# A triangular inverse whose blocks are turned on VectorE instead of through HBM, with a few mixture pieces moved into the next block

## The chip, the cores and the metric

The kernel runs on one core of a Trainium2 chip. The time is the device time of one execution in microseconds (us). The fast runs of one kernel in the same rounds lie 0.1 to 0.7% apart. Every run compared here is marked fast in the record (mean granted clock 0.932 to 0.963), or is the single run of a look without rounds, which is marked as such. The granted clock is the profile's figure for the share of full speed granted to TensorE; "slow clock" below means a stretch in which it is under 1 and the same work takes longer (0.68 over 518.9 to 525.6 us of the kernel before, where a ph piece takes 6.64 us instead of 4.51). Engines are named as in the profile: PE is TensorE's matmuls, PEld its weight loads, DVE is VectorE, ACT ScalarE, POOL GpSimd, SP SyncE; a name with q (SPq) is that engine's sequencer, for instance while it issues a transfer. "L481" is line 481 of the kernel that the profile belongs to, so the same code has other line numbers in other kernels.

## The reference

A recurrent attention (8 heads of 40, batch 4, 768 time steps) is followed by a mixture of four experts.

```python
for t in range(S):                                    # S = 768, per (batch, head)
    y[:, :, t] = einsum('bhd,bhde->bhe', r_t, state)
    Sa = einsum('bhde,bhe->bhd', state, a_t)
    state = state * w_t - einsum('bhd,bhe->bhde', Sa, b_t) + einsum('bhd,bhe->bhde', v_t, k_t)
x = y, as rows (B*S, H*D) = (3072, 320)
p = domain_probs / domain_probs.sum(-1)               # 4 experts
out = sum over e of  p[:, e] * (relu(x @ w1[e]) @ w2[e])    # w1: 320x1024, w2: 1024x320
```

## The kernel before

Time is cut into 12 chunks of 64 steps. Inside a chunk the recurrence is solved with a unit-triangular 64x64 inverse for each batch and head; state passes from chunk to chunk. The chunks are worked on in seven blocks (1, 2, 2, 2, 2, 2 and 1 chunks); a chunk has two units (half the batch each). A block does, in PE's order, which is the program's order (the scheduler orders the other engines; in e9 below pieces written ahead of the solve moved only one of VectorE's evictions):

1. per unit: turn the inputs (`pW`, `pNK`, `pKN`, `pA`, `pR`), make the triangles (`pef`), turn back (`pkn`);
2. `solve()`: up to 128 inverses of 32x32 triangles on VectorE, one per lane;
3. `inverse()`: join the 32x32 inverses to 64x64 ones (`pi`, `px`);
4. the steps of the chunks (`pa` ... `py`), and the result to HBM and back as `xT`.

The mixture of the block before is cut into pieces, `ph` (wide, x @ w1) and `po` (narrow, h @ w2), that are laid between these stages: `mix(us)` adds credit, and pieces run as far as the credit goes.

The triangles lie with rows on partitions, and `solve()` wants one triangle per lane. So they go through HBM:

```python
    def load(x, u):                    # the five inputs; each nat tile has ONE buffer
        ...
                nc.sync.dma_start(out=n[:, :, 0:D], in_=src[0].rearrange("h t e -> t h e"))
    def triangles(u):
        ...
            nc.scalar.copy(out=u.q.F[half(s), u.x], in_=cut(pef[s][half(s)]))
        ...
                nc.sync.dma_start(out=u.q.FD[s, z, ...].rearrange("m r t -> r m t"),     # to HBM
                    in_=blocks(u.q.F, s, z)[...])
    # in attention(), once the block's triangles are there:
                nc.sync.dma_start(out=Gl[u.q.lanes, 0:Q * Q], in_=u.q.FD[:]...)            # from HBM, by lanes
    def inverse(q, x):
        if x == 0:
            for y, t in enumerate((Xl, Tl)):
                nc.sync.dma_start(out=XD[y]..., in_=t[q.lanes, 0:Q * Q])                   # to HBM
            for s in range(2):
                for z in range(2):
                    nc.sync.dma_start(out=blocks(xt, s, z)[:, 0:n], in_=XD[0, s, z]...)    # from HBM, by rows
                nc.sync.dma_start(out=blocks(q.F, s, 0)[:, 0:n], in_=XD[1, s, 0]...)
        ...                                                                                # pi, px on TensorE

    def weights(e):                    # one buffer each for w1s and w2s
        ...
                nc.gpsimd.dma_start(out=w1s[half(d)], ...)
            nc.gpsimd.dma_start(out=w2s[:], ...)
    def narrow(e, tt):
        po = mbank("po")               # the mixture has four PSUM banks in turn
        ...                            # matmuls, then VectorE evicts po into osb

    def mix(us):
        if not queue and ahead:
            stage(*ahead.pop(0))
        credit[0] += us * credit[1]
        while queue and credit[0] >= queue[0][0] / 2:
            t, piece = queue.pop(0)
            credit[0] -= t
            piece()

    def attention(b):
        us = b.units
        stage(us[0], 1)                                  # decays: pW
        for y, u in enumerate(us):
            stage(u, 2)                                  # scaled: pNK, pKN, pA
            if y + 1 < len(us):
                stage(us[y + 1], 1)
            mix(4.3)
            stage(u, 3)                                  # triangles: pef
            mix(2.2)
            stage(u, 4)                                  # natural: pkn, pR
        ...
        solve(b.n * NP * 4 * M)
        mix(56)
        ...                                              # inverse, steps with mix, gather

    for y, b in enumerate(all_blocks):
        credit[:] = [0.0, sum(t for t, _ in queue) / 137]
        attention(b)
        mix(1e9)                                         # what is left of the mixture runs here
        queue += mixture(b.cs, b.xT)
    mix(1e9)
```

## Time and profile before

| | before |
|---|---|
| time, median of 3 runs | 1415.08 us (1414.68 to 1415.97) |
| span of the profiled run, TensorE's mean granted clock | 1413.4 us, 0.963 |
| busy: PE, DVE, ACT | 1255.5, 592.3, 262.8 us |
| moved by DMA | 135.75 MB |

PE's busy share, in tenths, in 40 equal slices of the span (35.3 us each):

```profile
PE   4167878978999978999978999979899979999998
```

The first nine slices are blocks 0 and 1, where PE waits most. After that each block shows one dip (7 or 8): the start of the block, where PE waits for the inputs. TensorE is 89% busy, so every gain has to come out of these dips or out of slow-clock stretches. The prediction shows the waits themselves.

### The profile page before, as it was taken

The numbers are of one execution on the slowest core, as the hardware profiler recorded it, in microseconds if no ns is written. First come the engines' busy times: TensorE is split into PE (matmuls) and PEld (weight loads), VectorE is DVE, ScalarE is ACT, GpSimd is POOL, SyncE is SP. The second block draws the span as 40 slices with busy tenths as digits, with TensorE's granted clock in tenths as the row PEclk, the third lists the DMA queues.
The fourth block names the chain that finished last, engine by engine and source line by source line (L and its number), as shares of the span: only waits on it lengthen the run. The fifth ranks groups of instructions, "written<-read, shape, count | busy, mean of one in ns | idle before, by whom it ended". The sixth has DMA issues, their size and how long they took to land.

```text
span 1413.4 us, 26645 instructions
## 1 busy us (share of the span) xinstructions
PE 1255.5 (89%) x11680; PEld 874.3 (62%) x11680; DVE 592.3 (42%) x877; ACT 262.8 (19%) x521; POOL 75.2 (5%) x108
## 2 busy tenths in 40 slices
PE   4167878978999978999978999979899979999998
PEld 4166656856557756557755657656557665566676
DVE  7744572345623345623345443345452335612000
ACT  1021212112121203111203112203113202120111
POOL 3000000000000000000000000000000000000010
PEclk9997988889999989999989999989999999999999
DMA  8233654456353446354445353354462353414363
GB/s 135 44 57 73 115 137 106 82 113 105 91 118 80 90 105 95 82 123 95 85 108 94 81 127 70 91 125 85 93 127 58 85 133 65 93 46 103 93 148 86
DMA packets 284020, 135.75 MB, mean 96 GB/s; under 512 B 246977, under 2 KB 265473, under 8 KB 283905
## 3 DMA queue, kind: packets, MB, share of 16 engines
q1 hardware_dynamic: 266304, 60.60, 24.6%
q0 software_dynamic: 17600, 73.46, 21.1%
q8 instruction: 92, 1.51, 0.5%
q14 instruction: 24, 0.19, 0.0%
HBM read 116.70 MB, written 17.30 MB: 95 GB/s over the span
## 4 chain that ended last, share of the span: by engine, by line
PE 70%; DMA 13%; DVE 10%; SPq 4%; issue 2%; ACT 1%; POOL 0%; DVEq 0%; ACTq 0%
PE ph L481 26%; PE po L493 23%; DVE tmp L288 3%; DMA natW<-in_w_dram 3%; PE pc L418 3%; PE pef L218 3%; DMA natKN<-in_b_dram 2%; DMA natA<-in_a_dram 2%; DMA w1s<-in_moe_w_dram 2%; SPq L162 2%; PE pa L379 2%; PE py L430 2%; PE pt L389 2%; PE py L436 1%; PE pSN L351 1%
## 5 line engine op out<-in xcount | busy, mean ns | idle before, releaser
L481 PE MATMUL ph<-xT,w1s 64*128 64x512 f32 (+1 forms) x2240 | 455.5, 553 | 18.1 <-DVE osb L502 8.1
L493 PE MATMUL po<-w2s,hs 128*128 128x320 f32 x1536 | 430.1, 437 | 0.0
L493 PEld LDWEIGHTS po<-w2s,hs 128*128 128x128 f32 x1536 | 289.4, 191 | 122.6 <-issue 8.5
L481 PEld LDWEIGHTS ph<-xT,w1s 64*128 64x128 f32 x2240 | 226.7, 196 | 210.1 <-issue 182.1
L487 ACT ACTIVATE hs<-ph 128x512 f32<-128x512 f32 (+1 forms) x224 | 110.4, 534 | 623.9 <-PE ph L481 623.0
L502 DVE SCALAR_TENSOR_TENSOR osb<-po,gate,osb 128x320 f32<-128x320 f32 x72 | 39.1, 549 | 370.1 <-PE po L493 370.1
L191 DVE RECIPROCAL GI<-G 128x512 f32<-128x512 f32 x24 | 80.5, 3353 | 0.8
L467 POOL DMA_DIRECT2D w1s<-in_moe_w_dram x56 | 37.8, 679 | 770.2 <-PE ph L481 770.2
L168 PE MATMUL pW<-ident,natW 128*128 128x128 f32 x96 | 18.6, 327 | 50.1 <-DMA natW<-in_w_dram 45.5
L329 PE MATMUL pi<-F 32*32 32x32 f32 x768 | 16.5, 199 | 47.0 <-DMA F<-XD 47.0
L218 PEld LDWEIGHTS pef<-AE,KNT 64*128 64x128 f32 x768 | 50.2, 199 | 12.6 <-issue 11.4
L471 POOL DMA_DIRECT2D w2s<-in_moe_w_dram x28 | 26.0, 928 | 545.7 <-PE po L493 545.7
L288 DVE TENSOR_TENSOR tmp<-Xl,Gl 128x1024 f32<-128x1024 f32 (+5 forms) x49 | 54.2, 1107 | 0.9
L225 DVE TENSOR_TENSOR AE<-pef,mask 64x512 f32<-64x512 f32 x48 | 33.1, 689 | 51.1 <-ACT F L223 50.3
L186 DVE TENSOR_TENSOR_SCAN G<-w_shift,first 128x520 f32<-128x520 f32 x24 | 29.8, 1242 | 56.1 <-ACT w_shift L184 55.9
L218 PE MATMUL pef<-AE,KNT 64*128 64x64 f32 x768 | 51.3, 283 | 2.2 <-DVE AE L205 2.1
L418 PEld LDWEIGHTS pc<-R,VST 64*128 64x128 f32 x768 | 47.8, 199 | 6.8 <-issue 4.2
L418 PE MATMUL pc<-R,VST 64*128 64x64 f32 x768 | 48.9, 284 | 2.0 <-DVE VST L357 1.4
L184 ACT COPY w_shift<-pW 128x512 f32<-128x512 f32 x24 | 14.0, 585 | 192.0 <-PE pW L168 189.5
L329 PEld LDWEIGHTS pi<-F 32*32 32x32 f32 x768 | 15.0, 115 | 52.0 <-issue 44.7
L168 PEld LDWEIGHTS pW<-ident,natW 128*128 128x128 f32 x96 | 13.1, 166 | 54.0 <-issue 48.1
L223 ACT COPY F<-pef 64x512 f32<-64x512 f32 x48 | 27.8, 580 | 99.5 <-PE pef L218 98.9
(104 smaller groups left out, 1013.7 us busy)
## 6 DMA issues: line engine op xcount, KB each, us to landing
w1s<-in_moe_w_dram POOLq DMA_DIRECT2D x56, 640.0 KB, 8.1
w2s<-in_moe_w_dram POOLq DMA_DIRECT2D x28, 1280.0 KB, 7.3
xT<-yD SPq DMA_DIRECT2D x24, 320.0 KB
natW<-in_w_dram SPq DMA_DIRECT2D x48, 80.0 KB
natA<-in_a_dram SPq DMA_DIRECT2D x48, 80.0 KB
natR<-in_r_dram SPq DMA_DIRECT2D x48, 80.0 KB
yD<-Yo SPq DMA_DIRECT2D x48, 80.0 KB
out_dram<-osb SPq DMA_DIRECT2D x48, 80.0 KB
```

What stands on the lines that cost most here:

```text
L168: nc.tensor.transpose(out=p[:, j * P:(j + 1) * P], in_=nat[x][:, 2 * j:2 * j + 2, :].rearrange("p h e -> p (h e)"), identity=ident[:],)
L191: nc.vector.reciprocal(out=u.GI[:], in_=u.G[:, :, 1:L + 1])
L218: nc.tensor.matmul(out=pef[s][:, m * L:(m + 1) * L], lhsT=KNT[half(s), m].rearrange("p x t -> p (x t)"), rhs=u.AE[half(s), s, m, :], start ...
L225: nc.vector.tensor_tensor(out=u.AE[o, s], in0=cut(pef[s][o]), in1=mask[o, None, :].to_broadcast([64, M, L]), op=ALU.mult,)
L288: nc.vector.tensor_tensor(out=m, in0=in0[:, :, None, :].to_broadcast([P, n0, n1, nr]), in1=in1[:, None, :, :].to_broadcast([P, n0, n1, nr] ...
L329: nc.tensor.matmul(out=p[hi, at], lhsT=f[lo, m, Q:L], rhs=f[lo, m, 0:Q], start=True, stop=True, tile_position=(SL[s], SL[s] + Q),)
L418: nc.tensor.matmul(out=pc[s][:, m * L:(m + 1) * L], lhsT=VST[half(s), i, j * P:(j + 1) * P], rhs=u.R[half(s), m, :], start=True, stop=True,)
L467: nc.gpsimd.dma_start(out=w1s[half(d)], in_=moe_w1[e, :, d * (F // 2):(d + 1) * (F // 2)].rearrange("(k p) f -> p k f", p=64),)
L481: nc.tensor.matmul(out=ph[d][:, 0:n], lhsT=w1s[half(d), k_, f * P:(f + 1) * P], rhs=xT[half(d), k_, 0:n], start=(k_ == 0), stop=(k_ == NK ...
L487: nc.scalar.activation(out=hs[-1][1][:, 0:n], in_=ph[d][:, 0:n], func=ACTF.Relu)
L493: nc.tensor.matmul(out=po[:, 0:DM], lhsT=h[:, tt * P:(tt + 1) * P], rhs=w2s[:, f, :], start=(x == 0), stop=(x == NF - 1),)
L502: nc.vector.scalar_tensor_tensor(out=osb[tt][:], in0=po[:, 0:DM], scalar=sc, in1=osb[tt][:], op0=ALU.mult, op1=ALU.add,)
```

## The change

Its intent is to take the four trips through HBM away. VectorE's transposition, as the changed kernel uses it, turns 32x32 blocks for every 32 partitions: with one triangle column per turn, it moves rows to lanes and back. `Tl`'s way back falls away, since F gets X as it is and XT gets it turned. Five other things came with it: the inputs KN and R of the first chunk are issued from ACT, the first weights wait for a tile of block 0, block 1's first two `decays` are written ahead of block 0's solve (before, all stages of these units were spread over block 0's steps), `VST` stands ahead of `pd` in a step, and not all mixture pieces run at the end of a block: some 13 us of them, three narrow pieces, stay for the next block. The core of the diff (renamings and the reshaping of `solve` are cut):

```diff
 def load(x, u):
+            by = nc.scalar if u.c == 0 and x in ("KN", "R") else nc.sync
 def triangles(u):
-            nc.scalar.copy(out=u.q.F[half(s), u.x], in_=cut(pef[s][half(s)]))
+            for z in range(2):
+                r = slice(SL[s] + z * Q, SL[s] + (z + 1) * Q)
+                nc.scalar.copy(out=F_[r, u.m, 0:L - z * Q], in_=cut(pef[s][r])[:, :, z * Q:L])
-        for s in range(2):
-            for z in range(2):
-                nc.sync.dma_start(out=u.q.FD[...], in_=blocks(u.q.F, s, z)[...])
+    def columns(t):
+        return t[:, :, 0:Q].rearrange("p m t -> p t m")
 def solve():
+        nc.vector.transpose(out=square(Gl), in_=columns(F_))
 ...
+        nc.vector.transpose(out=columns(F_), in_=X)
+        for z in range(2):
+            nc.vector.transpose(out=columns(XT[:, :, z * Q:L]), in_=X.rearrange("p r t -> p t r"))
+        for s in range(2):
+            nc.gpsimd.memset(XT[SL[s] + Q:SL[s] + L, :, 0:Q], 0.0)
 def inverse(u, x):
-        if x == 0:
-            ...                                       # XD to HBM and back
 def step(u, yD):                                      # VST moved ahead of pd
 def weights(e):
+            if cs[0] == e == 0:
+                for t in (w1s, w2s):
+                    nc.gpsimd.tensor_copy(out=t[:, 0, 0:1], in_=all_blocks[0].units[1].KNT[:, 0, 0, 0:1])
 def mix(us):
-        if not queue and ahead:
-            stage(*ahead.pop(0))
 def attention(b, after):
         if b.cs[0] == 0:
             ...
+            for u in after.units[0:NP]:
+                stage(u, 1)
-            ahead.extend((u, upto) for u in all_blocks[1].units[0:NP] for upto in range(1, 5))
 for y, b in enumerate(all_blocks):
-        mix(1e9)
+        credit[:] = [sum(t for t, _ in queue) - 13, 1.0]
+        mix(0)
         queue += mixture(b.cs, b.xT)
-    mix(1e9)
+    credit[0] = 1e9
+    mix(0)
```

More of the change, by code (lines that the diff above doesn't have):

```diff
@@ L115 @@
     VS = [const.tile([P, 2, NJ, 2, 64], FP32, name=f"VS{p}_") for p in range(NP)]
-    XT = [const.tile([P, 2, M, L], FP32, name=f"XT{p}_") for p in range(NP)]
+    F_ = const.tile([P, 2 * NP * M, L], FP32, name="F")
+    XT = const.tile([P, 2 * NP * M, L], FP32, name="XT")
     DG = 8 * (Q + 1)
     Xl, Tl, Gl = (const.tile([P, 4 * DG], FP32, name=x) for x in ("Xl", "Tl", "Gl"))
+    nc.gpsimd.memset(F_[:], 0.0)
+    for t in (Xl, Tl):
+        nc.gpsimd.memset(t[:], 0.0)
     def clear():
-        for t in (Xl, Tl):
+        for t in RV + VS:
             nc.gpsimd.memset(t[:], 0.0)
@@ L126, in clear @@
             nc.gpsimd.memset(t[:, Q + 1:Q + 1 + (Q - 1) * (Q + 1)].rearrange("p (a c) -> p a c", c=Q + 1)[:, :, 0:1], 1.0)
-        for t in XT + RV + VS:
-            nc.gpsimd.memset(t[:], 0.0)
     gate = const.tile([P, NC, NP, E], FP32, name="gate")
@@ L157, in load @@
             src = [y[2 * u.p + i, :, u.t, :] for y in srcs[x]]
+            by = nc.scalar if u.c == 0 and x in ("KN", "R") else nc.sync
             if srcs[x][0] is srcs[x][1]:
-                nc.sync.dma_start(out=n[:, :, 0:D], in_=src[0].rearrange("h t e -> t h e"))
+                by.dma_start(out=n[:, :, 0:D], in_=src[0].rearrange("h t e -> t h e"))
                 continue
             for s in range(2):
-                nc.sync.dma_start(out=n[:, s::2, 0:D], in_=src[s][s::2].rearrange("h t e -> t h e"))
+                by.dma_start(out=n[:, s::2, 0:D], in_=src[s][s::2].rearrange("h t e -> t h e"))
     def turn(x):
@@ L209, in triangles @@
     def triangles(u):
-        KNT, q = u.KNT, u.q
-        if q.F is None:
-            q.F = sb.tile([P, 2, M, L], FP32, name="F", tag="F", bufs=2)
-            q.FD = hbm.tile([2, 2, q.n * M, Q, Q], FP32, name="FD", tag="FD", bufs=4)
+        KNT = u.KNT
         pef = [bank("pef") for _ in range(2)]
@@ L227, in triangles @@
             )
-        for s in range(2):
-            for z in range(2):
-                nc.sync.dma_start(
-                    out=u.q.FD[s, z, u.x * M:(u.x + 1) * M].rearrange("m r t -> r m t"),
-                    in_=blocks(u.q.F, s, z)[:, u.x * M:(u.x + 1) * M],
-                )
     def natural(u):
@@ L249, in natural @@
         nc.scalar.copy(out=u.R[:], in_=cut(turn("R")[:]))
-    def blocks(t, s, z):
-        o = SL[s] + z * Q
-        return t[o:o + Q].rearrange("p c m t -> p (c m) t")[:, :, z * Q:(z + 1) * Q]
     def square(t):
@@ L260, in eights, with solve @@
     def eights(t):
-        return t.rearrange("p (x m) -> p x m", m=DG)[:, :, 0:8 * Q].rearrange("p x (a c) -> p x a c", c=Q)
-    def solve(P):
-        Xp, Tp, Gp = Xl[0:P], Tl[0:P], Gl[0:P]
-        X8, G8 = eights(Xp), eights(Gp)
-        X, T, Ft = square(Xp), square(Tp), square(Gp).rearrange("p r t -> p t r")
-        tmp = sb.tile([128, 1024], FP32, name="tmp", tag="tmp", bufs=1)[0:P]
+        return t[:].rearrange("p (x m) -> p x m", m=DG)[:, :, 0:8 * Q].rearrange("p x (a c) -> p x a c", c=Q)
+    def columns(t):
+        return t[:, :, 0:Q].rearrange("p m t -> p t m")
+    def solve():
+        nc.vector.transpose(out=square(Gl), in_=columns(F_))
+        X8, G8 = eights(Xl), eights(Gl)
+        X, T, Ft = square(Xl), square(Tl), square(Gl)
+        tmp = sb.tile([128, 1024], FP32, name="tmp", tag="tmp", bufs=1)
         for t in range(1, 8):
@@ L272, in solve @@
             nc.vector.tensor_tensor(
-                out=m, in0=X8[:, :, 0:t, 0:t], in1=G8[:, :, 0:t, t:t + 1].rearrange("p x r o -> p x o r").to_broadcast([P, 4, t, t]), op=ALU.mult,
+                out=m, in0=X8[:, :, 0:t, 0:t], in1=G8[:, :, t:t + 1, 0:t].to_broadcast([P, 4, t, t]), op=ALU.mult,
             )
@@ L296, in solve @@
             for o in range(0, Q, 2 * n):
-                Y = sb.tile([128, 16, 16], FP32, name="Y", tag="Yl", bufs=1)[0:P]
+                Y = sb.tile([128, 16, 16], FP32, name="Y", tag="Yl", bufs=1)
                 for i in range(2):
@@ L305, in solve, with inverse @@
                          T[:, o + n + i * h:o + n + (i + 1) * h, o + n:o + n + nr], negate=True)
-                nc.vector.tensor_copy(
-                    out=T[:, o + n:o + 2 * n, o:o + n], in_=X[:, o:o + n, o + n:o + 2 * n].rearrange("p a c -> p c a"),
-                )
-    def inverse(q, x):
-        xt = XT[q.p]
-        n = q.n * M
-        if x == 0:
-            XD = hbm.tile([2, 2, 2, n, Q, Q], FP32, name="XD", tag="XD", bufs=4)
-            for y, t in enumerate((Xl, Tl)):
-                nc.sync.dma_start(out=XD[y].rearrange("s z m r t -> (s z m) (r t)"), in_=t[q.lanes, 0:Q * Q])
-            for s in range(2):
-                for z in range(2):
-                    nc.sync.dma_start(out=blocks(xt, s, z)[:, 0:n], in_=XD[0, s, z].rearrange("m r t -> r m t"))
-                nc.sync.dma_start(out=blocks(q.F, s, 0)[:, 0:n], in_=XD[1, s, 0].rearrange("m r t -> r m t"))
-        f, xt = q.F[:].rearrange("p c m t -> p (c m) t"), xt[:].rearrange("p c m t -> p (c m) t")
+                if n == 8:
+                    nc.vector.tensor_copy(
+                        out=T[:, o + n:o + 2 * n, o:o + n], in_=X[:, o:o + n, o + n:o + 2 * n].rearrange("p a c -> p c a"),
+                    )
+        nc.vector.transpose(out=columns(F_), in_=X)
[3 more added lines that the diff above has]
+            nc.gpsimd.memset(XT[SL[s] + Q:SL[s] + L, :, 0:Q], 0.0)
+    def inverse(u, x):
+        f, xt = F_[:, u.m], XT[:, u.m]
         p = bank("pi" if x == 0 else "px")
-        for m in range(n):
+        for m in range(M):
             at = slice(m * Q, (m + 1) * Q)
@@ L340, in inverse @@
             if x == 0:
-                nc.scalar.copy(out=f[hi, 0:n, 0:Q], in_=cut(p[hi, 0:n * Q], Q))
+                nc.scalar.copy(out=f[hi, :, 0:Q], in_=cut(p[hi, 0:M * Q], Q))
             else:
-                nc.scalar.mul(out=xt[lo, 0:n, Q:L], in_=cut(p[lo, 0:n * Q], Q), mul=-1.0)
+                nc.scalar.mul(out=xt[lo, :, Q:L], in_=cut(p[lo, 0:M * Q], Q), mul=-1.0)
     def across(name, t):
@@ L360, in step @@
     def step(u, yD):
-        rv, vs, xt = RV[u.p], VS[u.p], XT[u.p][:, u.x]
+        rv, vs, xt = RV[u.p], VS[u.p], XT[:, u.m]
         bs = slice(2 * u.p, 2 * u.p + 2)
@@ L399, in step @@
         yield 4.3
+        VST = across("VST", vs)
+        yield 0
         if u.c != NC - 1:
@@ L412, in step @@
                 nc.vector.tensor_tensor(out=x, in0=x, in1=decay[rows(s)].to_broadcast([D, 2, NJ, D]), op=ALU.mult)
-        yield 0
-        VST = across("VST", vs)
         yield 4.3
@@ L515, in block @@
         n = len(cs)
-        qs = [Of(p=p, n=n, lanes=slice(p * n * 4 * M, (p + 1) * n * 4 * M), F=None) for p in range(NP)]
-        return Of(n=n, cs=cs, qs=qs, units=[
-            Of(c=c, x=x, p=p, q=qs[p], t=slice(c * L, (c + 1) * L), at=0) for x, c in enumerate(cs) for p in range(NP)
+        return Of(n=n, cs=cs, units=[
+            Of(c=c, p=p, t=slice(c * L, (c + 1) * L), at=0, m=slice((x * NP + p) * M, (x * NP + p + 1) * M))
+            for x, c in enumerate(cs) for p in range(NP)
         ])
@@ L525, in stage @@
             (decays, scaled, triangles, natural)[u.at - 1](u)
-    queue, ahead, credit = [], [], [0.0, 1.0]
+    queue, credit = [], [0.0, 1.0]
     def mix(us):
-        if not queue and ahead:
-            stage(*ahead.pop(0))
         credit[0] += us * credit[1]
@@ L537, in mix, with attention @@
             piece()
-    def attention(b):
+    def attention(b, after):
         us = b.units
@@ L549, in attention @@
             stage(u, 4)
-            if u.x == b.n - 1:
-                nc.sync.dma_start(
-                    out=Gl[u.q.lanes, 0:Q * Q], in_=u.q.FD[:].rearrange("s z m r t -> (s z m) (r t)"),
-                )
         if b.cs[0] == 0:
@@ L556, in attention @@
             gates()
+            for u in after.units[0:NP]:
+                stage(u, 1)
         early.clear()
-        solve(b.n * NP * 4 * M)
+        solve()
         mix(56)
         for x in range(2):
-            for q in b.qs:
-                inverse(q, x)
+            for u in us:
+                inverse(u, x)
             mix(4.3)
-        if b.cs[0] == 0:
-            ahead.extend((u, upto) for u in all_blocks[1].units[0:NP] for upto in range(1, 5))
         b.xT = mo.tile([P, NK, 2 * B * L], FP32, name="xT", tag="xT", bufs=2)
@@ L580 @@
         credit[:] = [0.0, sum(t for t, _ in queue) / 137]
-        attention(b)
-        mix(1e9)
+        attention(b, all_blocks[min(y + 1, len(all_blocks) - 1)])
+        credit[:] = [sum(t for t, _ in queue) - 13, 1.0]
+        mix(0)
         queue += mixture(b.cs, b.xT)
-    mix(1e9)
+    credit[0] = 1e9
+    mix(0)
 _INS = ["r", "k", "v", "w", "a", "b", "moe_domain_probs", "moe_w1", "moe_w2"]
```

## The prediction

Cut from the text below is what was set for each transposition, four in a solve and two named among block 1's terms. The sum came to 74.6 us won (35.6 + 38 + 1), so 1340.5, said as 1341; it and the times stated behind the cuts (34.5, 70.8, 72.0, 74.4, 76.0, 109 to 110, 179.5, 182 and what follows from them) still contain the cut terms. The 2.5 us of rival (2) is the author's estimate: the 60% beside it is measured (1950 against 1224 ns), the 2.5 is not.

> **What bounds the kernel now.** I read the page's clock and chain, then TensorE's waits, then the chain in order of time, then the timelines of one middle block. There are seven blocks of time chunks (1, 2, 2, 2, 2, 2, 1 chunks); each block's attention is interleaved on TensorE (PE) with the mixture of the block before. The chain:
>
> ```profile
> PE 70%; DMA 13%; DVE 10%; SPq 4%; issue 2%; ACT 1%; POOL 0%; DVEq 0%; ACTq 0%
> ```
>
> and the waits of PE (total us, times, longest):
>
> ```profile
> PE pi L329 <- DMA F<-XD: 47.0, 9, 37.2
> PE pW L168 <- DMA natW<-in_w_dram: 45.5, 10, 8.4
> PE pA L168 <- DMA natA<-in_a_dram: 8.6, 4, 4.2
> ```
>
> So PE work is 70% of the path, and the time to win is in PE's waits: 47.0 us for the inverse's blocks to come back from HBM (F<-XD, 37.2 of it in block 0), and 45.5 us for natW. Where the stages lie in the chain of time (first column start, second length, us):
>
> ```profile
> 16.59 13.17 DMA natKN<-in_b_dram
> 40.62 3.08 DMA Gl<-FD
> 72.25 1.95 DMA XD<-Xl
> 77.05 2.08 DMA XD<-Tl
> 80.04 2.04 DMA F<-XD
> 85.20 3.57 PE pa L379 x64
> ...
> 171.56 3.40 DMA Gl<-FD
> 205.17 3.78 DMA XD<-Tl
> 211.07 3.16 DMA XD<-Tl
> 215.98 2.20 DMA F<-XD
> ```
>
> Only blocks 0 and 1 show the HBM trips together with the solve between them (VectorE, 43.8 to 72.6 and 175.0 to 205.0). From block 2 on the chain at that place is PE ph and po: the 56 us of mixture laid over the solve hide it. PE was busy 61.3 of the first 131.25 us, 142.2 of the next 173.0, and 203 of about 215 in each block after that. A middle block loses its 12 us here (PE, then the SP queue):
>
> ```profile
> 517.89 1.09 PE L168 MATMUL pW<-ident,natW 128*128 128x128 f32 x4 [7.79 <-DMA natW<-in_w_dram]
> 518.91 6.64 PE L481 MATMUL ph<-xT,w1s 64*128 64x512 f32 x20
> ...
> 560.93 1.09 PE L168 MATMUL pKN<-ident,natKN 128*128 128x128 f32 x4 [2.92 <-DMA natKN<-in_b_dram]
> ```
>
> ```profile
> 509.52 1.46 SPq L508 DMA_DIRECT2D out_dram<-osb  x2
> 511.03 0.71 SPq L159 DMA_DIRECT2D natW<-in_w_dram  x1
> ```
>
> The tiles nat* have one buffer. The second unit's natW can be fetched only after the first unit's transposition, which comes after the last mixture piece; it then takes 6.1 us to land (511.74 to 517.89), because the last mixture matmul has just released the next 1.28 MB of w2s.
>
> [...] the ph piece after the 7.79 us gap takes 6.64 instead of 4.51 us; even the 2.92 us gap doubles the next pKN (1.09 against 0.60 for the same four elsewhere).
>
> **The change, part by part.**
>
> *Solve.* Gl now arrives transposed, so its reads are contiguous. By shapes, tmp<-Xl,Gl 128x1024 takes 1950 ns (rows strided), tmp<-Y,Tl of the same size 1224. Saved: 3 x 0.73 = 2.2, plus 2 x (595-424) + 2 x (382-292) = 0.5, about 0.4 in the seven small steps, 0.4 for the last copy to Tl, which goes: 3.5 us. 29.1 becomes 25.6. Four transpositions are added, 1 before and 3 after[...]. Per solve the DMA chains go: FD, Gl in, XD, F back.
>
> *Block 0.* The first unit is bound by the mask copy on VectorE (2.57 to 9.1, behind the memsets), the scan and the 3.35 us reciprocal; that stays, pef at 17.35. For the second unit the natKN wait (13.17) shrinks: KN and R are issued from ScalarE, and the weights wait for the second KNT. Loads land by about 14, so PE's order decides: pR of unit 0 ends at 23.8, three turns of 0.9, VectorE 1.4, pef from 28.0 to 31.5 (was 37). F is evacuated in four copies, 1.9; transposed, 34.5. The old solve began at 43.8: 9.3 won. But in the new order of VectorE the scans and reciprocals of block 1's first two units stand inside this solve: 2 x (1.24+3.35) = 9.2, plus 1.5 waiting for w_shift. 34.5+10.7+25.6 = 70.8 (was 72.6). F at 72.0, XT at 74.4; pi, px, pa at 76.0 (was 85.2). From there the rest of block 1's preparation, which used to run between the steps, is gone. Summed from durations: pa 3.6, pSN 3.8, pt 2.7, VS 1.4, pVST 2.1, pd 1.6, pc 4.3, CX (behind four updates of RV) 2.2, py and Yo 3.0, yD and natNK issues 4.0, xT 5.5: 34, giving ph at 109 to 110 (was 131.25). **22 us won.**
>
> *Block 1.* It must now do all four units' preparation. PE work from first ph to the last pef: four ph 10.6, po 4.4, four pef 7.8, pkn/pR 5.1, turns 5.2: 33 us, plus 6 us because the next w1s burst falls on the last unit's natKN and natA, as it did at 147.8 to 157.5. So the last pef ends at 149 (was 166.8). F 1.9, [...]solve 25.6+0.5[...] F ready at 179.5. PE has 30.5 us of mixture to do and arrives then too. pi ends at 182 (was 220.1): the former tail of 51.5 us from pef to pi is 33. Given back: on POOL the zeroing of XT stands ahead of the third w2s, so w2s lands at about 191.3 and PE waits 4.7 plus 1.9 of slow clock. The rest (225.9 to 295.3, less one po piece moved on, 4.4, plus 1 for slow clock) takes it to 257.3. The new start gap and the moved piece bring it to 268.6, against 304.2. **35.6 won in all up to here.**
>
> *Blocks 2 to 5.* The HBM trips were hidden, so their removal alone wins nothing. Two gaps shrink. (a) natW: the mixture pieces that used to precede the gap now follow it, so the w2s burst comes later; natW follows yD in the queue: issued at 1.6 to 2.9 us after the last py, landing 2.2 later (the unloaded latency at 542.8 to 545). PE has 2.2 us to do, so it waits 3 rather than 7.8. The slow clock after it stays. That is 4.5. (b) With the four FD writes gone (1.8 to 5 us of SP time per unit) a unit needs 9.1 us of issue against PE's 11 to 13, and the w1s burst moves behind the stages: 2.9 to 4.2 of wait and 1.8 of slow clock go, 1 us may remain: 4. Small waits (F<-XD 0.5, others) 1. **9.5 x 4 = 38.**
>
> *Last block and tail.* Bound by PE (241.0 busy of 247.6): 1.
>
> Sum: 35.6 + 38 + 1 = 74.6; 1415.1 - 74.6 = 1340.5. I say 1341.
>
> **Rivals.** (1) The start gap only moves: natW now queues behind yD, which waits for the last Yo, and the three pieces stand behind the second pW in PE's order, so they cannot fill that wait. For it: [...]the new order shows exactly this. Against it: natW took 6.1 us under the w2s burst and about 2.2 without. If the landing stays at 6, (a) is lost: 18 us, 1359. (2) Strided transpositions cost 2.5 us or more each, as strided reads cost 60% more above: about 5 us in block 0 and up to 5 in block 1, nothing later: 1350. (3) POOL: XT's memset in the weights' queue delays a burst in every block. From block 2 on I find the memset done 3 us or more before w1s is needed; if that is wrong, 5 us a block: 1361. (4) A better outcome: if the w1s burst misses block 1's loads, another 6 us; and if the pieces do cover the gap, 5 x 4: 1320. That the whole gain vanishes needs (1) and (b) failing together with block 0: the 40 us at pi in block 0 and 1 speak against it.
>
> **Range and chances.** The wins of blocks 0 and 1 rest on several chained waits (35.6, plausibly 25 to 45); those of the middle on one latency and one queue (38, plausibly 18 to 50). Together 1320 to 1370. Faster by over 2% means under 1386.8, so so within 2% means less than 28 of the 74.6 realized: 5%. Slower by over 2% would take a wait in every block that I do not see: 1%. The rest, 94%, is faster.
>
> **What would show it.** Right: no F<-XD; [...]first ph near 109; pi of block 1 near 180; pW's wait near 3 us at each start of a block; no wait for natKN or natA over 1.5 in blocks 2 to 5; period 206. Wrong: pW waiting 7 us or more; PE waiting for w1s or w2s behind the memset of XT; transpositions over 2.5 us; a first ph later than 118.

## The result, and the profile after

The changed kernel takes **1391.8 us** (median of 4 runs, 1390.9 to 1395.3) against 1415.5 us of the kernel before in the same rounds: ratio 0.984, 95% interval 0.982 to 0.986. Ratios here and below are the mean time of one kernel's fast runs over that of the other's of the same rounds, so not quite the ratio of the medians quoted. The gain is clear of the noise, but it is 23.7 us where the prediction said 74, and the time is outside the predicted range. With a threshold of 2% the verdict is "same", an outcome that the prediction gave 5%. Seven later kernels, which keep the transposition and alter only where or on which queue something stands in the program, come within the range; the best takes 1348.6 us.

PE by slices after (34.7 us each), and the shares of the chain that ended last:

```profile
PE   5076779999999989999989999989999989899998
```

```profile
PE 74%; DVE 13%; DMA 6%; issue 5%; ACT 1%; SPq 1%; POOL 0%; DVEq 0%; POOLq 0%; ACTq 0%
```

DMA fell from 13% of the chain to 6%, DVE rose from 10 to 13. The waits of PE (us in total, times, longest):

```profile
PE pi L325 <- DVE F L310: 32.1, 1, 32.1
PE pW L176 <- DMA natW<-in_w_dram: 29.4, 10, 9.3
PE ph L481 <- DVE osb L502: 9.4, 1, 9.4
...
PE ph L481 <- DMA w1s<-in_moe_w_dram: 7.7, 5, 5.6
PE pKN L176 <- issue: 7.5, 2, 4.1
...
PE ph L481 <- DVE osb L500: 6.8, 3, 2.3
PE pKN L176 <- DMA natKN<-in_b_dram: 5.8, 2, 3.4
```

The 47.0 us for F<-XD are gone; in their place 32.1 us stand at the one solve that nothing covers, block 0's. natW fell from 45.5 to 29.4. But w1s rose from 1.6 us and osb L500 from 0.7, and natKN is still there: 5.8 us, and 7.5 more at the same place in blocks 3 and 5, which the profile puts down to "issue" (before: 5.9 and 3.1). The 9.4 us for osb L502, in block 1, were 8.1 before.

Where the 24.1 us between the two spans came from can be read at the pW that has waited for natW, near the start of a block; the prediction cut its sum there too (its 304.2 us, and its tail of 247.6 us, lie one instruction later). Some mixture work is still to do at those moments in the new kernel; it is set right here (one piece of 4.4 us at block 2, three of together 13.1 at block 6).

| stretch | before | after | won | predicted |
|---|---|---|---|---|
| start to the end of block 2's wait for natW | 303.1 | 276.7 + 4.4 | 22.0 | 35.6 |
| from there to the end of block 6's wait for natW | 861.6 | 842.2 + 8.7 | 10.7 | 38 |
| from there to the end | 248.6 | 270.4 - 13.1 | -8.6 | 1 |

So the loss is in all three, and most of it in the middle blocks, in which nothing of the transposition lies on the path.

**A middle block.** From the timeline of PE in block 4 (start us, length us, what, the idle time before it and its releaser):

```profile
689.14 0.74 PE L176 MATMUL pW<-ident,natW 128*128 128x128 f32 x4 [3.30 <-DMA natW<-in_w_dram]
689.67 6.09 PE L493 MATMUL po<-w2s,hs 128*128 128x320 f32 x16
...
705.09 4.47 PE L493 MATMUL po<-w2s,hs 128*128 128x320 f32 x16
...
718.03 1.08 PE L176 MATMUL pKN<-ident,natKN 128*128 128x128 f32 x4 [3.42 <-DMA natKN<-in_b_dram]
...
721.35 5.68 PE L481 MATMUL ph<-xT,w1s 64*128 64x512 f32 x20
...
772.79 13.14 PE L481 MATMUL ph<-xT,w1s 64*128 64x512 f32 x58 [2.29 <-DVE osb L500]
```

and from POOL and SP in the same stretch:

```profile
709.86 0.93 POOL L471 DMA_DIRECT2D w2s<-in_moe_w_dram  x1 [36.18 <-PE po L493]
```

```profile
710.14 0.61 SPq L170 DMA_DIRECT2D natKN<-in_b_dram  x1
```

natW at the block's start makes PE wait 3.30 us, where it was 7.79 in the old block that the prediction shows: that step held. But the third left-over po ends at 709.5, frees the single w2s, and the next 1.28 MB of weights are asked for at 709.86, in the very microseconds in which SP issues the four parts of the third unit's natKN (708.19 to 710.75; the last is shown). That natKN is late by 3.42 us, and what follows the gap runs at the slow clock (0.50 granted over 718.0 to 719.2, 0.80 over 721.3 to 727.1; the ph at 721.35 takes 5.68 us, 4.51 elsewhere). Further on, four po in a row overtake VectorE, which is in the solve, and ph waits 2.29 us for a PSUM bank. The last part of natKN is issued at 710.14 and PE goes on at 718.03, 7.9 us later; from 715.0 to 720.0 the profile gives a DMA share of 1.09 and 203 GB/s. That POOL's load of w2s delays SP's small one is read from this overlap, and from e1 and e7 below, where w2s is asked for at another time and PE does not wait for natKN in this block.

### The profile page after: what moved, and what is told of

It is laid out like the page before. It is cut to its first block, busy times and chain, and to the rows that moved or that the text cites. A ratio compares the mean times of both kernels' runs of the same rounds, so it can differ in the third digit from the quotient of the medians.

```text
span 1389.3 us, 26523 instructions
## 1 busy us (share of the span) xinstructions
PE 1250.1 (90%) x11680; PEld 869.5 (63%) x11680; DVE 624.7 (45%) x898; ACT 283.9 (20%) x609; POOL 88.7 (6%) x123
## 4 chain that ended last, share of the span: by engine, by line
PE 74%; DVE 13%; DMA 6%; issue 5%; ACT 1%; SPq 1%; POOL 0%; DVEq 0%; POOLq 0%; ACTq 0%
PE ph L481 27%; PE po L493 23%; DVE tmp L287 3%; PE pef L223 3%; PE pc L414 3%; DMA natW<-in_w_dram 3%; DMA w1s<-in_moe_w_dram 2%; PE py L426 2%; DVE Y L291 2%; PE pa L375 2%; PE pSN L347 2%; PE py L432 2%; PE pt L385 2%; PE pVST L347 2%; DVE Xl L291 1%
## 5 line engine op out<-in xcount | busy, mean ns | idle before, releaser
L493 PE MATMUL po<-w2s,hs 128*128 128x320 f32 x1536 | 435.0, 441 | 0.0
L481 PEld LDWEIGHTS ph<-xT,w1s 64*128 64x128 f32 x2240 | 223.7, 193 | 223.7 <-issue 194.6
L502 DVE SCALAR_TENSOR_TENSOR osb<-po,gate,osb 128x320 f32<-128x320 f32 x72 | 39.5, 550 | 339.5 <-PE po L493 339.1
L230 ACT COPY F<-pef 32x512 f32<-32x512 f32 x96 | 45.1, 469 | 102.2 <-PE pef L223 101.0
L353 DVE COPY SN<-pSN 128x512 f32<-128x512 f32 x24 | 16.6, 692 | 108.4 <-PE pSN L347 108.4
L232 DVE TENSOR_TENSOR AE<-pef,mask 64x512 f32<-64x512 f32 x48 | 33.1, 689 | 64.9 <-ACT F L230 64.6
L223 PE MATMUL pef<-AE,KNT 64*128 64x64 f32 x768 | 51.5, 282 | 5.0 <-DVE KNT L210 3.5
L176 PE MATMUL pW<-ident,natW 128*128 128x128 f32 x96 | 18.8, 330 | 34.8 <-DMA natW<-in_w_dram 29.4
L414 PEld LDWEIGHTS pc<-R,VST 64*128 64x128 f32 x768 | 44.9, 188 | 5.6 <-issue 4.1
L414 PE MATMUL pc<-R,VST 64*128 64x64 f32 x768 | 45.7, 272 | 1.1 <-DVE RV__99 L407 1.1
L325 PE MATMUL pi<-F 32*32 32x32 f32 x768 | 14.2, 195 | 32.1 <-DVE F L310 32.1
L420 DVE TENSOR_TENSOR CX<-pc,mask 128x512 f32<-128x512 f32 x48 | 30.7, 686 | 27.3 <-PE pc L414 27.2
L437 DVE TENSOR_TENSOR Yo<-py,G 128x512 f32<-128x512 f32 x24 | 16.6, 692 | 53.2 <-PE py L432 53.2
```

Source lines behind the costliest of these rows:

```text
L223: nc.tensor.matmul(out=pef[s][:, m * L:(m + 1) * L], lhsT=KNT[half(s), m].rearrange("p x t -> p (x t)"), rhs=u.AE[half(s), s, m, :], start ...
L230: nc.scalar.copy(out=F_[r, u.m, 0:L - z * Q], in_=cut(pef[s][r])[:, :, z * Q:L])
L414: nc.tensor.matmul(out=pc[s][:, m * L:(m + 1) * L], lhsT=VST[half(s), i, j * P:(j + 1) * P], rhs=u.R[half(s), m, :], start=True, stop=True,)
L481: nc.tensor.matmul(out=ph[d][:, 0:n], lhsT=w1s[half(d), k_, f * P:(f + 1) * P], rhs=xT[half(d), k_, 0:n], start=(k_ == 0), stop=(k_ == NK ...
L493: nc.tensor.matmul(out=po[:, 0:DM], lhsT=h[:, tt * P:(tt + 1) * P], rhs=w2s[:, f, :], start=(x == 0), stop=(x == NF - 1),)
L502: nc.vector.scalar_tensor_tensor(out=osb[tt][:], in0=po[:, 0:DM], scalar=sc, in1=osb[tt][:], op0=ALU.mult, op1=ALU.add,)
```

## The experiments

First a summary; "left" is the number of pieces that stay for the next block, "period" the time from the first pi of block 3 to that of block 4 and from 4 to 5.

| kernel | left | median us | ratio to before, 95% | period |
|---|---|---|---|---|
| before | 0 | 1415.5 | | 215.0, 216.8 |
| changed | 3 | 1391.8 | 0.984 (0.982 to 0.986) | 214.8, 214.9 |
| e1_left1 | 1 | 1363.5 | 0.965 (0.961 to 0.968) | 208.1, 208.8 |
| e2_left0 | 0 | 1388.1 | 0.981 (0.979 to 0.983) | 211.4, 211.2 |
| t1_transposes_only | 0 | 1385.4 | 0.979 (0.977 to 0.982) | 212.1, 211.4 |
| b1_left3 | 3 | 1431.5 | 1.011 (1.009 to 1.014) | 225.2, 222.6 |
| e35_gate_zero | 3 | 1386.7 | 0.979 (0.977 to 0.981) | 214.8, 215.1 |
| e6_decays_later | 3 | 1383.5 | 0.976 (0.974 to 0.979) | 214.7, 215.1 |
| e9_mix_first | 3 | 1391.6 | 0.983 (0.981 to 0.985) | 214.8, 215.0 |
| t2_dense (one run) | 3 | 1400.5 | | 214.9, 215.0 |
| e7_three_early | 3 | 1356.0 | 0.959 (0.957 to 0.960) | 204.8, 205.3 |
| c1_left1_decays | 1 | 1357.4 | 0.958 (0.956 to 0.961) | 205.6, 206.8 |
| c2_mix_before | 1 | 1355.1 | 0.956 (0.953 to 0.960) | 207.7, 208.4 |
| c4_t1_left1 | 1 | 1360.4 | 0.961 (0.960 to 0.963) | 207.8, 204.6 |
| f1_early_decays | 3 | 1348.6 | 0.954 (0.951 to 0.956) | 205.2, 206.9 |
| f2_xt_after_mix | 3 | 1350.0 | 0.956 (0.953 to 0.959) | 204.6, 205.8 |

All gave the right result. Each ratio is to the kernel before in the same rounds (its medians: 1414.0 to 1415.7 us). Where two of the other kernels are compared below, it is by medians of different rounds, except among e1, e2, t1 and b1, among e35, e6 and e9, among e7, c1, c2 and c4, and between f1 and f2.

### How many pieces are left: e1_left1 and e2_left0

The theory was that the left-over pieces do the harm. The rival was that their number hardly matters.

```diff
-        credit[:] = [sum(t for t, _ in queue) - 13, 1.0]
+        credit[:] = [sum(t for t, _ in queue) - 4, 1.0]      # e1: one piece left
+        credit[:] = [sum(t for t, _ in queue) - 0, 1.0]      # e2: none left
```

> The changed kernel (1391.8 us), but about one mixture piece (4.3 us) is left for the next block instead of three (13 us). Theory (weight burst): with three pieces the next expert's 1.28 MB w2s load is released in the middle of the preparation and lands on the third unit's natKN, as at 709.9 in the changed kernel (3.4 to 4.1 us of wait and 2.6 of slow clock in blocks 3 to 5), and four po pieces in a row under the solve cost 2.3 us of waiting for osb; with one piece, as block 2 has it now, both go: 6 to 8 us a block in three blocks, of which the last block gives 5 to 9 back because w1s is then needed earlier while the zeroing of XT still holds up its load: 1372 to 1384. Rival (SP queue: the natKN wait is the in-order queue's issue time, whatever the bursts): natKN waits stay at 3 us or more, 1388 to 1395.

> The changed kernel with no piece left for the next block (all are flushed before it, as in the old kernel). Theory (burst): the w2s burst falls on natW again, so pW waits 7 us or more at each block start instead of 3.3; natKN's wait goes in blocks 3 to 5; near the changed kernel, 1385 to 1400. Rival (what shortened the natW wait was its new place in the queue, not the pieces): pW waits stay near 3.3 and the time falls under 1380.

One piece: 1363.5 us, below the range of the theory (1372 to 1384). The miss is in the last block, which was to give back 5 to 9 us and won 6.2; block 4 won 6.8 us, as the theory had it. None: 1388.1 us, as expected, with 51.9 us of waits for natW. The instant at which POOL asks for the next w2s, counted from block 4's first pW, says why: with none left 0.5 us, beside the second unit's natW (issued at 0.6 and 2.6; PE waits 7.66 us for it); with three 26.0 us, in the midst of the third unit's natKN (issued from 24.3 to 26.9); with one 13.5 us, between the two, and neither is late by much (natW 3.84, natKN 0). The rival, SP's issue time, falls: SP does issue one transfer after the other, 0.59 to 2.81 us for each line of its timeline (704.07 to 721.92 in the changed kernel), but it has issued natKN 3.9 us before PE is ready for it in the changed kernel and 4.2 us in e1, nearly the same, and only in the changed kernel does it land late.

### The transposition alone, and the pieces alone: t1_transposes_only and b1_left3

```diff
 # t1: the changed kernel, with all but the transposition path as before
-            by = nc.scalar if u.c == 0 and x in ("KN", "R") else nc.sync     # loads on SP
-                    nc.gpsimd.tensor_copy(out=t[:, 0, 0:1], in_=...KNT...)   # no gate for weights
-            for u in after.units[0:NP]: stage(u, 1)                           # block 1 prepared in the steps again
+            ahead.extend(...)
         VST = across("VST", vs)                                               # behind pd again
+        mix(1e9)                                                              # nothing left over
 # b1: the kernel before, with three pieces left
-        mix(1e9)
+        credit[:] = [sum(t for t, _ in queue) - 13, 1.0]
+        mix(0)
```

> The old kernel with the transposition path alone: loads, weights' start, order of VST, flush of the pieces and preparation in block 0 as before. Theory: blocks 0 and 1 win about 10 us each, the middle blocks 0 to 3 each because the HBM trips were hidden, the last block loses about 10 to w1s behind the zeroing of XT: 1393 to 1408. Rival (the FD writes cost the middle blocks their natKN wait): the natKN waits of 3 to 4 us vanish in blocks 2 to 5 and the time is under 1390.

> The old kernel with only three mixture pieces left for the next block. Theory: the natW wait falls from 7.7 to 3 to 5 us at the block starts, but the natKN wait stays or grows through the moved w2s burst: 1403 to 1415. Rival (the pieces are what the change gains in the middle blocks): 1395 or less.

The transposition alone is worth 30 us, more than the whole change: the rival's side, since the waits for natKN and natA, 2.9 to 4.2 us in the old middle blocks, all but went (2.5 and 2.6 us in the whole kernel, at most 1.0 in blocks 2 to 5). That the FD writes were what held these loads up is likely but not shown: t1 takes all trips through HBM away together. Its first ph comes at 122.0 us, not 113.3, but by block 1's pi it is ahead (202.6 against 206.4): what the changed kernel wins in block 0 by not preparing block 1 there, it pays back in block 1. The pieces alone make the old kernel slower by 16 us (1.1%, clear of the noise); I had expected them to be harmless or useful there, which was wrong. natW's wait fell to 3.4 us at the longest, as it should, but ph waited eight times for osb evictions at L500, 16.2 us in all (0.7 before).

### Two small waits of the changed kernel: e35_gate_zero

In block 6 alone does PE wait for weights because the zeroing of XT holds them up on POOL (POOL, then PE):

```profile
1175.31 1.94 POOL L314 MEMSET XT<- 32x1024 f32 x2 [35.17 <-DVE XT L312]
1177.20 1.35 POOL L467 DMA_DIRECT2D w1s<-in_moe_w_dram  x2
```

```profile
1160.56 17.49 PE L493 MATMUL po<-w2s,hs 128*128 128x320 f32 x64
1183.69 2.04 PE L481 MATMUL ph<-xT,w1s 64*128 64x512 f32 x2 [5.64 <-DMA w1s<-in_moe_w_dram]
```

The last ph before these po had freed w1s at 1160.6, yet its reload was issued at 1177.20, behind a memset that had waited 35 us for the solve. And in block 0's solve the first burst of weights, now released at 24.6 us, delays natW of block 1's second unit (PE waits 9.3 us for it at 42.52, 4.0 in the run below).

```diff
-            nc.gpsimd.memset(XT[SL[s] + Q:SL[s] + L, :, 0:Q], 0.0)
+            nc.vector.memset(XT[SL[s] + Q:SL[s] + L, :, 0:Q], 0.0)
-        ... in_=all_blocks[0].units[1].KNT[:, 0, 0, 0:1])
+        ... in_=all_blocks[1].units[1].G[:, 0, 0:1])
```

> The changed kernel with two small alterations in different stages: XT's zeroing stands on VectorE, not POOL, and the first weights burst is released by G of block 1's second unit, not by KNT of block 0. Theory (the zeroing on POOL holds up w1s only in block 6, for 5.6 + 1.1 us and 2.2 us of slow ph; the burst released at 24.6 us delays natW of block 1 by about 5 us inside block 0's solve): the wait PE ph <- w1s at 1177 to 1185 us goes, the VectorE gap of 5.1 us before G at 44 us shrinks below 2 us, and the time falls by 8 to 14 us, to 1377 to 1385. Rival (both waits are replaced at once: w1s by TensorE work that it hides behind, natW by VectorE, which is the bound there): within 3 us of 1391.8.

1386.7 us, 5.1 less, just short of the theory's range. Both waits went. The gate brought pi of block 0 forward by 5.8 us, but the osb wait in block 1 grew from 9.4 to 11.8, and by block 5's pi only 2.0 us were left. The zeroing won 6.2 us in block 6.

### The decays inside block 0's solve: e6_decays_later

VectorE in block 0's solve of the changed kernel:

```profile
33.83 1.24 DVE L194 TENSOR_TENSOR_SCAN G<-w_shift,first 128x520 f32<-128x520 f32 x1
...
35.11 3.35 DVE L199 RECIPROCAL GI<-G 128x512 f32<-128x512 f32 x1
...
44.26 1.24 DVE L194 TENSOR_TENSOR_SCAN G<-w_shift,first 128x520 f32<-128x520 f32 x1 [5.13 <-ACT w_shift L192]
```

These three, a second reciprocal of 3.35 us behind them and the wait of 5.13 us, 14.3 us in all, stand in the one solve that nothing covers.

```diff
             gates()
-            for u in after.units[0:NP]:
-                stage(u, 1)
         early.clear()
         solve()
         ...                                  # mix, inverse
+        if b.cs[0] == 0:
+            for u in after.units[0:NP]:
+                stage(u, 1)
```

> The changed kernel with block 1's two decays moved from the front of block 0's solve to after its inverse. Theory (VectorE sets the end of block 0's solve, and 2 x (1.24 + 3.35) + 5.1 us of foreign work and wait stand in it): pi of block 0 begins 9 to 14 us earlier than before the alteration, and the time falls by 5 to 12 us, to 1380 to 1387. Rival (the decays were off the path or only move the wait to block 1's start, where pW of the next units waits for the single natW): pi of block 0 is earlier, but the start of block 2 is not, and the time is 1389 to 1396.

pi of block 0 at 62.0 instead of 75.7, the first ph at 105.7 instead of 113.3, and the time 8.3 us lower, 1383.5: the theory.

### Evictions ahead of the solve: e9_mix_first

In block 1, PE waits 9.4 us for osb. PE, then VectorE, of the changed kernel:

```profile
198.60 7.87 PE L481 MATMUL ph<-xT,w1s 64*128 64x256 f32 x40 [9.36 <-DVE osb L502]
```

```profile
192.22 1.90 DVE L310 STREAM_TRANSPOSE F<-Xl 128x1024 f32<-128x1024 f32 x1
193.98 4.14 DVE L312 STREAM_TRANSPOSE XT<-Xl 128x1024 f32<-128x1024 f32 x2
198.03 0.96 DVE L502 SCALAR_TENSOR_TENSOR osb<-po,gate,osb 128x320 f32<-128x320 f32 x2
```

```diff
-        solve()
         mix(56)
+        solve()
```

> The changed kernel with the mixture pieces that run under the solve written ahead of the solve, so that the scheduler sees the osb evictions first; in the resulting order of VectorE only one of them moves, in one block, ahead of the two XT transpositions. Theory (in block 1 TensorE waits 9.4 us at ph because the osb evictions stand behind XT's transpositions on VectorE): the wait there falls by 2 to 5 us and the time by as much, to 1386 to 1390. Rival (the wait is replaced by pi waiting for F, since the same VectorE work ends at the same moment): 1390 to 1394.

1391.6 us: no change. The wait split into two of together 8.6 us, since only one eviction moved. The rival's number came out, but not for the rival's reason.

### What a transposition costs: t2_dense

```diff
         nc.vector.transpose(out=square(Gl), in_=columns(F_))
+        for _ in range(2):
+            nc.vector.transpose(out=square(tmp0), in_=square(Gl))
```

> The changed kernel with two further 128x1024 transpositions in each solve, both sides of them dense (Gl to tmp), whose result is not used. If the length of a transposition comes from its element count alone, they last as long as the strided ones, 1.9 to 2.1 us each[...]. The time grows by 7 x 2 x that, where the solve is bare on the path (blocks 0 and partly the others): 3 to 20 us.

The groups of VectorE in that kernel (busy us, mean ns of one):

```profile
L315 DVE STREAM_TRANSPOSE XT<-Xl 128x1024 f32<-128x1024 f32 x14 | 29.4, 2145 | 0.0
L269 DVE STREAM_TRANSPOSE tmp<-Gl 128x1024 f32<-128x1024 f32 x14 | 17.4, 1241 | 0.4
L313 DVE STREAM_TRANSPOSE F<-Xl 128x1024 f32<-128x1024 f32 x7 | 13.6, 1940 | 0.2
L265 DVE STREAM_TRANSPOSE Gl<-F 128x1024 f32<-128x1024 f32 x7 | 13.5, 1930 | 0.0
```

Both sides dense: 1.24 us. One strided side (steps of 256 bytes in F): 1.93 to 1.94, 0.7 more. Both strided (256 bytes in XT, 128 in Xl): 2.15, another 0.2. Size, type and operation are the same, so in this kernel the strides make the difference, not the element count; why they do was not shown.

### The moment or the number: e7_three_early

e1 and e2 could be read in two ways: three pieces are too many, or they end at the wrong moment. This kernel keeps three and runs them at once in the first gap of the preparation. They are no longer charged to `credit`, which is set from the other pieces alone (those lines are cut).

```diff
             if y + 1 < len(us):
                 stage(us[y + 1], 1)
+            if y == 0:
+                for _ in range(b.left):        # the number of pieces left over
+                    queue.pop(0)[1]()
             mix(4.3)
```

> The changed kernel with its three left-over pieces kept, but run together in the first gap of the next block's preparation, ahead of the first pef, not spread over three gaps. Theory (what costs is the moment at which the last left-over piece frees w2s and lets the next burst of weights collide with natKN of the third unit, about 3.5 us of wait and 2.5 us of slow clock in each of blocks 3 to 5): the natKN waits of 3.4 to 4.1 us in these blocks fall below 1.5 us, the period from pi to pi falls from 214.8 to 208 to 212 us, and the time is 1368 to 1382. Rival (what costs is to have three pieces rather than one, because of the evictions that line up or of the TensorE work that is missing from the end of the block): the period stays at 213 us or above and the time at 1384 or above.

1356.0 us, 35.8 less than the changed kernel, better than the theory's range. The same place as in the block shown above (PE, then POOL):

```profile
680.82 0.63 PE L176 MATMUL pW<-ident,natW 128*128 128x128 f32 x4 [3.25 <-DMA natW<-in_w_dram]
681.28 13.09 PE L493 MATMUL po<-w2s,hs 128*128 128x320 f32 x48
...
717.32 0.60 PE L176 MATMUL pKN<-ident,natKN 128*128 128x128 f32 x4
```

```profile
694.66 0.93 POOL L471 DMA_DIRECT2D w2s<-in_moe_w_dram  x1 [29.25 <-PE po L493]
```

Counted from the block's first pW (675.60 here, 683.88 in the changed kernel), w2s is asked for at 19.1 us instead of 26.0, and the third unit's natKN is issued from 34.9 us on instead of 24.3, as PE comes to that unit later. So 15.9 us lie between the two, and by an estimate w2s has landed, at about 703, before natKN is issued (from 710.54): the issue ends at 695.6, and the changed kernel's page gives w2s a median of 7.1 us to landing. PE no longer waits for natKN in blocks 2 to 5, nor does ph for osb. Of the 10.0 us that the changed kernel takes longer from block 4's first pW to block 5's (214.82 against 204.83), PE's busy time makes 5.0 (204.67 against 199.73: the same matmuls, at the clock granted 0.96 and 1.00 in the block's preparation and solve) and idle time the other 5.0 (3.4 of it natKN, 2.3 osb). So it is where the pieces stand that costs, not their number. How much of the 10.0 us comes from w2s meeting natKN alone, no run isolates, since the osb waits went with the same edit.

### Together: c1_left1_decays, c2_mix_before, c4_t1_left1, f1_early_decays, f2_xt_after_mix

c1 is e1 with e6's diff. c2 is c1 with the first mixture piece ahead of the next unit's pW:

```diff
+            mix(4.3)
             if y + 1 < len(us):
                 stage(us[y + 1], 1)
-            mix(4.3)
```

c4 is t1 with e1's diff. f1 is e7 with e6's diff. f2 is f1 with XT's two transpositions and the zeroing moved from the end of `solve()` to behind `mix(56)`.

> One left-over piece and block 1's decays after block 0's inverse: the two alterations that helped, together. If they add up (1363.5 less 8.3): 1353 to 1358. If the second is swallowed by waits of the first: 1360 to 1365.

> As the run before, and the first mixture piece of each preparation stands ahead of the next unit's pW, not behind it. Theory (the wait PE pW <- natW of 3.3 to 3.8 us at the start of blocks 2 to 6 has nothing in front of it, and one piece of 4.5 us would cover it): these five waits go, and the time is 1338 to 1347, some 13 to 18 us below the run before. Rival (the wait moves to the G and KNT that need pW, and PE waits there instead): 1350 to 1360.

> The kernel before with the transposition path and one left-over piece; loads, weights' start, prepared units and the order of VST as before. It tells whether the remaining parts of the change (loads on ACT's queue, decays inside the solve of block 0, earlier weights, VST moved) are worth anything: if the transposition and one piece are all that pays, 1355 to 1367, as the changed kernel with one piece (1363.5); if the other parts are worth what the prediction gave them in block 0 (8 to 10 us), 1371 to 1376.

> The three left-over pieces run early and block 1's decays after block 0's inverse, together. If the two costs are separate, as the theory says (36 us lost by the moment of the left-over pieces, 8 by the decays inside the solve): 1346 to 1351, and 5 to 10 us are left to the 1341 of the prediction. If they overlap: 1353 to 1357.

> As the run before, with XT's two transpositions written behind the mixture pieces that run under the solve. Theory (the 9.4 us wait PE ph <- osb in block 1 is the eviction standing behind F's and XT's transpositions on VectorE; without XT's 4.1 us ahead of it, it comes 4 us earlier): the wait falls to about 5.3 us and the time by 3 to 5 us against the run before, to 1342 to 1347. Rival (pi is bound by F and px then waits for XT in the other blocks, so nothing is won, or the zeroing on POOL, which moves with it, holds up weights): 1347 to 1353.

- c1: 1357.4 us, in the range of "they add up".
- c2: 1355.1 us. natW's wait fell to 10.0 us in the whole kernel, but pR <- KN (8.6 us, 6 times) and pef <- KNT (8.4, 6 times) came in its place: the rival.
- c4: 1360.4 us. The transposition and one piece are all that pays; the loads on ACT, the earlier weights, the decays in the solve and the order of VST are worth nothing in sum (e1, which has them all, takes 1363.5).
- f1: **1348.6 us, the fastest version**, 65 us under the kernel before in its rounds (1414.0) and 43 under the changed one; 35.8 and 8.3 had been won singly, so they add up.
- f2: 1350.0 us, the same as f1 within the scatter. VectorE's order there shows why:

```profile
185.94 0.48 DVE L506 SCALAR_TENSOR_TENSOR osb<-po,gate,osb 128x320 f32<-128x320 f32 x1
186.34 4.19 DVE L316 STREAM_TRANSPOSE XT<-Xl 128x1024 f32<-128x1024 f32 x2
190.44 0.51 DVE L506 SCALAR_TENSOR_TENSOR osb<-po,gate,osb 128x320 f32<-128x320 f32 x1
```

The first eviction now comes ahead of XT, the next one behind it, and the wait is 5.3 and 3.3 us, 8.6 together instead of 9.3. No run has taken this wait away.

## Why the prediction was wrong

The direction was right; the size was wrong by 51 us (50.5 between the spans): 13.6 up to block 2's wait for natW, 27.3 from there to block 6's, 9.6 at the end.

**Blocks 2 to 5, the step that failed most.** The prediction's (a), natW waiting 3 us instead of 7.8, came true (3.2 to 3.4). Its (b) failed as the prediction put it: "the w1s burst moves behind the stages: 2.9 to 4.2 of wait and 1.8 of slow clock go". It looked at w1s and at SP's issue time, and t1 shows that for the transposition alone this is right. But it did not ask where the *other* burst goes when the pieces move: w2s is freed by the last left-over po, and with three pieces spread over three gaps that po ends in the middle of the preparation, on natKN of the third unit (3.4 to 4.1 us of wait in blocks 3 to 5, where 1 was allowed). (b)'s gain was given back there, and 2.3 us of osb wait that I had not counted came on top. With the pieces early (e7), the same kernel wins 38.6 us in this stretch (861.6 against 814.4 + 8.7) where the prediction had 38, at a period of 204.8 to 206.4 where it had 206. So the sum came out for another placement of the pieces, which was not the one predicted. That the placement is what was missed is shown by that run; that w2s meeting natKN is the larger part of it is read from the traces.

**The last block.** Rival (3), POOL's memset in the weights' queue, was dismissed from block 2 on; that holds for blocks 2 to 5 and fails in block 6: 5.6 + 1.1 us of w1s wait, and e35 makes them go. The memset does this only together with the late pieces: in e7 it still stands on POOL, but it is done 8 us before w1s is asked for, PE waits 0.9 us for w1s in the whole kernel, and this stretch loses 1.0 us, not 8.6.

**Block 0.** pef and the start of the solve came as predicted (33.8 against 34.5). The solve without foreign work took 25.6 us, as worked out. Two terms were mis-sized: the wait for w_shift inside the solve was 5.1, not 1.5, because the first weights, released early, meet natW (issued at 25.1 to 27.4; the DMA share is 1.08 over 30 to 35 us and 1.00 over 35 to 38, and an 80 KB natW issued by 36.27 took 6.2 us to land; in e35, which releases them later, PE waits 4.02 us for that natW, here 9.34); and each transposition took 1.9 to 2.1 us, more than the prediction had set for it. Rival (2) named strides, but its estimate for them was 2.5 us. F was ready at 75.6 (72.0 predicted), the first ph at 113.3 (109 to 110). The decays were booked as a given, 10.7 us; e6 shows that the kernel is better by 8.3 us without them there.

**Block 1.** Last pef at 161.4 instead of 149 us: 4 of it from block 0; the rest because four units in a row waited for natKN, natA, natW and for VectorE for 10.2 us in all, plus slow clock (0.50 granted over 147.8 to 149.0), where 6 had been allowed. Then a term that was missing: evictions of osb stand behind F's and XT's transpositions in VectorE's order, and PE waits 9.4 us at ph. The old trace had this wait already (8.1 us in block 1, at the end of the solve), so it was there to be read. In the other direction, the w2s wait of 6.6 us that was booked behind the memset of XT didn't occur in this block, and from pi's end on it took 64.9 us to the end of block 2's first turns instead of 75.3.

**Smaller readings.** What the prediction set for a transposition fits dense sides (1.24, t2), not the strided ones of the change. It sets slow work beside the idle gap before it (7.79 and 2.92 us), but in these traces the length of a gap alone doesn't tell whether what follows is slow: after 2.92 us four pKN turns took 1.09 us instead of 0.60 (kernel before, 560.93; clock 0.50 over 560.9 to 562.1), after only 2.43 us the same (changed kernel, 147.85; 0.50 over 147.8 to 149.0), after 3.30 us a po took 6.09 (changed kernel, 689.67; 0.73 over 689.6 to 695.8), but after 3.25 us three took 13.09, 4.36 each (e7, 681.28; 1.00 over 675.6 to 798.4). Its "tail of 51.5 us" is 53.3 by its own two times (166.8 to 220.1); the sum does not use it.

**What is left.** f1 removes the two big terms and stands at 1348.6, 8 us above the predicted 1341. The 9.4 us osb wait is of that size, but as no run removed it, that it is the rest is argued, not shown. Why three pieces cost the old kernel as much as 16 us (b1) was not followed beyond its waits for osb.

## What to carry to other kernels

When work moves, ask which single buffer its last instruction frees, and what the transfer that this starts will meet: here 36 us hung on where three pieces of 13 us stood, and with them on whether a 1.28 MB load was asked for in the midst of a small one or 16 us ahead of it. Do not put deferred work where it ends beside small urgent loads (natKN 3.4 us late in a middle block here), and do not put the next stage's work into the one stretch that nothing covers (8.3 us in e6). And test the parts of a change one by one: here one part was worth more than the whole.
